# Gradient of the KV cache in a decode kernel: products over 64 rows and 512 columns per matmul instead of 32 rows and 256

One Trainium2 (trn2) chip, one core. The metric is the device time of one execution in microseconds (us), lower is better; a figure quoted for a kernel is the median of its runs.

## The reference

Two layers of grouped-query attention over a long cache alternate with two MLP layers, for two sequences of one token each, forward and backward. Ten outputs are asked: the result and the gradients of the input, the two caches and the weights.

```python
B, Sq, D = 2, 1, 1024
Hq, Hkv, Sk, Dh = 32, 4, 16384, 128          # 8 query heads per cache head

q = (x @ wq).reshape(B, Sq, Hq, Dh)...
scores = einsum("bhqd,bhkd->bhqk", q, k) * Dh ** -0.5
p = softmax(scores);  o = einsum("bhqk,bhkd->bhqd", p, v)
# ... wo, MLP; the same two layers twice with the same weights and caches
out, vjp = jax.vjp(f, x, k_cache, v_cache, wq, wo, w1, b1, w2, b2)
return (out, *vjp(grad_out))
```

What matters here: for each of the 8 pairs of sequence and cache head ("group", `g`), dV is P^T dO and dK is dS^T q, with 16 rows to sum over (2 layers x 8 heads) and 16384 tokens to produce. dK and dV together are 67 MB to write.

## The kernel before

Most loads of the caches and the weights, the forward pass and the first part of the backward pass come first, to about 733 us. The main loop after it loads another 50 of the 226 pieces of 1 MB of the caches, computes, for chunks of 32 tokens x 128 partitions, dS of the first layer and the gradients of K and V, and works off the weight gradients in the gaps.

The coefficients of dV and dK (`e_all` and `dX`) are transposed into `blk`: 128 rows are 4 pairs of tokens x (2 layers x 8 heads x 2 tokens). So 32 rows hold the coefficients of one pair of tokens. The moving operand `Qm` is block-diagonal: for each of two tokens 16 rows of q (or dO) in 128 columns, and zeros elsewhere. One matmul of 32 rows and 256 columns then gives two tokens of 128 numbers for 128 partitions. `Qm` is made at each new group: DVE spreads the columns of q into a scratch tile `spr`, two matmuls by the identity transpose it, and a copy takes it out of PSUM.

```python
    for w in "VK":
        spr[w] = wrk.tile([128, 258], BF16, name="spr" + w)
        nc.gpsimd.memset(spr[w][:], 0.0)

    def q_make(w, g, bank):
        Qm = wrk2.tile([128, 2, 128], BF16, name="Qm" + w)
        for t in range(2):
            PE.matmul(bank[:, t * 128:(t + 1) * 128], lhsT=spr[w][:, t * 128:(t + 1) * 128], rhs=ident[:],
                      start=True, stop=True)
        evac_cast(Qm[:].rearrange("p a b -> p (a b)"), bank[:, 0:256], 256)
        qms[w, g] = Qm
    # ... cut
    def make_qm(w, g):
        q_spread(w, cols[w][:, g].rearrange("p l r -> p (l r)"), 0, 16)    # DVE, at once
        return lambda: q_make(w, g, mx())                                  # PE and copy, later in the pass
    # ... cut
    def kv_pair(w, i, h):                    # half a chunk of dV or dK: 0.5 MB
        # ... cut
        pss = [mx() for _ in range(4)]       # the four PSUM banks that all such work shares
        for b in range(2):
            for r in range(4):
                PE.matmul(pss[r][:, b * 256:(b + 1) * 256], lhsT=blk[32 * r:32 * r + 32, o + 2 * h + b, :],
                          rhs=Qm[32 * r:32 * r + 32, :, :].rearrange("p a b -> p (a b)"), start=True, stop=True,
                          tile_position=(32 * r, 0))
        for r in range(4):
            evac_cast(sv_[:, 2 * h:2 * h + 2, r], pss[r][:].rearrange("p (b t d) -> p b t d", b=2, t=2), 512)
        # ... store
    # ... cut: the main loop, one pass
        for w, i in (("V", iv), ("K", ik)):
            if i is not None and chunks[i][1] == 0 and (w, chunks[i][0]) not in qms:
                qs.append(make_qm(w, chunks[i][0]))
        for k in range(2):
            ...                              # transpose, score block, one kv_pair
        for f in qs:
            f()
```

`evac_cast` gives a copy to ACT or DVE, whichever has less charged to it. In the orders of time shown below the copies and matmuls of an engine start in the order of the program (at the new group at 771.39 us, say, DVE's multiplication for dX starts at 772.05, the copy behind it at 772.64 and V's spreading at 773.24). A new group falls in every eighth pass, for V and K in the same pass, seven times in the loop.

Of the kernel before, what the change touches and what calls it, by code (L numbers as in the profile page):

```python
# [9 lines left out]
BF16 = mybir.dt.bfloat16  # L10
F32 = mybir.dt.float32
# [12 lines left out]
def kernel(  # L24
# [24 lines left out]
    nc = tc.nc  # L49
    V = nc.vector  # L50
    S = nc.scalar
    PE = nc.tensor
# [9 lines left out]
    FJ = F // 128  # L62
# [23 lines left out]
    wrk = ctx.enter_context(tc.tile_pool(name="wrk", bufs=1))  # L86
    wrk2 = ctx.enter_context(tc.tile_pool(name="wrk2", bufs=2))
# [20 lines left out]
    ident = const.tile([128, 128], BF16, name="ident")  # L108
# [25 lines left out]
    def charge(eng, us):  # L134
        load[eng] += us
# [7 lines left out]
    def pick():  # L143
        if only["e"]:
            return only["e"]
        m = min(load.values())
        for k in load:
            load[k] -= m
        return "A" if load["A"] <= load["D"] else "D"
# [9 lines left out]
    def evac_cast(dst, src, n):  # L159
        if pick() == "A":  # L160
            S.copy(out=dst, in_=src)  # L161
            charge("A", 0.17 + n / 1200.0)
        else:
            V.tensor_copy(out=dst, in_=src)  # L164
            charge("D", 0.15 + n / 960.0)
# [636 lines left out]
    def mlp_slope(l):  # L802
        sv = saved[f"m{l}"]
        hpre, th = sv["hpre"], sv["th"]
        t2 = wrk.tile([128, FJ, 2], F32, name="gb_t2")
        V.tensor_tensor(out=t2[:], in0=th[:], in1=th[:], op=ALU.mult)
        V.tensor_scalar(out=t2[:], in0=t2[:], scalar1=-1.0, scalar2=1.0, op0=ALU.mult, op1=ALU.add)
        x2 = wrk.tile([128, FJ, 2], F32, name="gb_x2")
        V.tensor_tensor(out=x2[:], in0=hpre[:], in1=hpre[:], op=ALU.mult)
        V.tensor_scalar(out=x2[:], in0=x2[:], scalar1=3.0 * GELU_A * GELU_C * 0.5, scalar2=GELU_C * 0.5,  # L810
                        op0=ALU.mult, op1=ALU.add)
        V.tensor_tensor(out=x2[:], in0=x2[:], in1=hpre[:], op=ALU.mult)
        V.tensor_tensor(out=x2[:], in0=x2[:], in1=t2[:], op=ALU.mult)
        d1 = sv["d1"] = vec.tile([128, FJ, 2], F32, name=f"gb_d1{l}")
        V.tensor_scalar(out=d1[:], in0=th[:], scalar1=1.0, scalar2=0.5, op0=ALU.add, op1=ALU.mult)
        V.tensor_tensor(out=d1[:], in0=d1[:], in1=x2[:], op=ALU.add)
# [105 lines left out]
    x3 = attn_layer_fwd(1, x2_)  # L922
    mlp_hidden(1, x3)
    mlp_slope(1)

    mlp_hidden_bwd(1, dh_up1)
# [16 lines left out]
    def some(q, n):  # L943
        for _ in range(n):
            if q:
                q.popleft()()

    mlp_slope(0)
    copies_on("A")
    g2 = attn_in_bwd(1, g3, dn1, lambda: some(rest, 2), lambda: some(rest, 3))  # L950
# [60 lines left out]
    cols = {}  # L1011
# [4 lines left out]
                V.tensor_copy(out=cols[w][:, :, k, :], in_=saved["a%d" % k]["qT_bf" if w == "K" else "doT_bf"][:])  # L1016
    g0_ = order[0]
    qms, spr, wide_do = {}, {}, {}
    for w in "VK":
        spr[w] = wrk.tile([128, 258], BF16, name="spr" + w)  # L1020
        nc.gpsimd.memset(spr[w][:], 0.0)

    def q_spread(w, gcols, k0, n):
        diag = spr[w][:].rearrange("p (t x) -> p t x", x=129)[:, :, 0:128].rearrange(
            "p t (r k z) -> p t r k z", r=4, k=16)[:, :, :, k0:k0 + n, 0]
        for t in range(2):
            V.tensor_copy(out=diag[:, t], in_=gcols.unsqueeze(1).to_broadcast([128, 4, n]))

    def q_make(w, g, bank):
        Qm = wrk2.tile([128, 2, 128], BF16, name="Qm" + w)  # L1030
        for t in range(2):
            PE.matmul(bank[:, t * 128:(t + 1) * 128], lhsT=spr[w][:, t * 128:(t + 1) * 128], rhs=ident[:],
                      start=True, stop=True)
        evac_cast(Qm[:].rearrange("p a b -> p (a b)"), bank[:, 0:256], 256)
        qms[w, g] = Qm

    def q_parts():
        q_spread("K", cols["K"][:, g0_].rearrange("p l r -> p (l r)"), 0, 16)
        q_make("K", g0_, px([128, 512], F32, "qk0"))
        q_spread("V", cols["V"][:, g0_, 1, :], 8, 8)  # L1040
        V.tensor_copy(out=wide_do[g0_][:, 8:16, 3], in_=cols["V"][:, g0_, 1, :])
# [77 lines left out]
    def nxt(what, lst):  # L1119
        rot[what] += 1  # L1120
        return lst[(rot[what] - 1) % len(lst)]

    def mx():
        return nxt("x", X)
# [4 lines left out]
    def new_home():  # L1129
        return (by_read or by_store).popleft()  # L1130
# [6 lines left out]
    def store(out_ap, view, tile_):  # L1137
        pace["queue"].dma_start(out_ap, view)
        if tile_ is not None:
            by_store.append(tile_)  # L1140
# [98 lines left out]
    late, late_pe = deque(), deque()  # L1239

    def make_qm(w, g):
        q_spread(w, cols[w][:, g].rearrange("p l r -> p (l r)"), 0, 16)
        return lambda: q_make(w, g, mx())

    stgs, split = {}, {}

    def kv_pair(w, i, h):

        g, c = chunks[i]
        if h == 0:  # L1250
            stgs[w, i] = new_home()
        sv_ = stgs[w, i][:].rearrange("p (b r t d) -> p b r t d", r=4, t=2, d=128)
        blk, Qm = blks[w, i], qms[w, g]
        o = 0 if w == "V" else NB
        pss = [mx() for _ in range(4)]
        for b in range(2):
            for r in range(4):
                PE.matmul(pss[r][:, b * 256:(b + 1) * 256], lhsT=blk[32 * r:32 * r + 32, o + 2 * h + b, :],  # L1258
                          rhs=Qm[32 * r:32 * r + 32, :, :].rearrange("p a b -> p (a b)"), start=True, stop=True,
                          tile_position=(32 * r, 0))  # L1260
        for r in range(4):
            evac_cast(sv_[:, 2 * h:2 * h + 2, r], pss[r][:].rearrange("p (b t d) -> p b t d", b=2, t=2), 512)
        if h == 0:
            split[w, i] = pace["short"] or i >= NC - 2
        if h == 1 or split[w, i]:
            lo = h if split[w, i] else 0
            dst = (dVv if w == "V" else dKv)[g, :, c * TC + lo * TC // 2:c * TC + (h + 1) * TC // 2, :]
            store(dst, stgs[w, i][:, lo * LDW // 2:(h + 1) * LDW // 2].rearrange("p (t d) -> p t d", d=128),
                  stgs[w, i] if h == 1 else None)
# [123 lines left out]
    dl_bank = delta_mm(0, dof, pt([128, 512], F32, "dl"), halves[1])  # L1393
    q_spread("V", dof[:, g0_], 0, 8)
    q_make("V", g0_, mx())
    V.tensor_copy(out=wide_do[g0_][:, 0:8, 3], in_=dof[:, g0_])
    odp = {1: kept_scores(1, sm_dp())}
    do_scaled(0, pairs(dops, HQ), dof, wob, (0,))
    delta(0, dl_bank, halves[1])
    charge("D", 1.0)  # L1400
    kv_pair("V", 0, 0)
    odp[0] = kept_scores(0, tp_dp())
    for c in (1, 0):
        ds0(c, odp[c])
    kv_pair("V", 0, 1)
    odp[2] = kept_scores(2, tp_dp())
    for q in range(4):
        dq_quad(1 - q // 2, q % 2)
    odp[3] = kept_scores(3, sm_dp())
    for c in (2, 3):  # L1410
        ds0(c, odp[c])
    kv_pair("V", 1, 0)
    for q in range(4):
        dq_quad(2 + q // 2, q % 2)
# [19 lines left out]
    while 2 * m < NS + 2:  # L1434
# [4 lines left out]
# [4 lines that stand above are left out]
            s = 2 * m + k  # L1443
            if s < NS:
                i, b = NCH + s // NB, s % NB
# [16 lines left out]
            at, w, m_ = ((k_at, "K", m - 1), (v_at, "V", m))[k]  # L1462
# [21 lines left out]
    i, g = NC - 1, order[-1]  # L1484
# [58 lines left out]
```

## Time and profile before

| | before |
|---|---|
| time, first three runs | 1142.25 us (1141.24 to 1142.84) |
| span of the profiled run | 1136.9 us |
| PE / DVE / ACT busy | 944.5 / 633.7 / 564.7 us |
| moved by DMA | 449.31 MB |
| calls of `kv_pair` | 128, from 733.5 to 1121.5 us |
| loop, passes 0 to 14 (14 passes; the engines set the pace) | 86.6 us |
| loop, passes 14 to 54 (40 passes; memory is full) | 256.4 us |
| from pass 54 to the end | 49.4 us |

The page of a profile describes one execution. The busy time of an engine says how long it had anything in hand, not that it was the limit: matmuls overlap in the trace (the eight of the call at 1018.53 us start within 130 ns and take 267 to 279 ns each). The row of GB/s against its own highest value, 425, is the better view of memory. A pass begins where the first transpose of its score block starts. Lines named L1258 and so on are lines of the kernel; the copies of all PSUM banks carry the lines of their helper, L161 on ACT and L164 on DVE.

One caution for all that follows: the profiled execution of the kernel before was a quick one. It took 1138.65 us, 3.6 less than the median and less than each of the runs in the table, so its stretches may be a few us short.

### The profile page before, as it was taken

Reading aid. Unit: us, or ns where it says so; the run is one execution under the profiler, and the core shown is the slowest. Engines: PE = TensorE matmul, PEld = TensorE weight load, DVE = VectorE, ACT = ScalarE, POOL = GpSimd, SP = SyncE. Lnnn points to the kernel's source line nnn. Section 1 sums busy time; section 2 is a strip of 40 time slices with the busy share of each in tenths; the row PEclk is TensorE's granted clock in tenths of the full one; section 3 lists DMA queues with packets and bytes.
Section 4 is the critical chain, followed back from the end, with each engine's and each line's share of the span. In section 5 each row is a group of like instructions: output and inputs, shape, how many; then the busy total and the mean of one; then the engine's idle time right before and its main releaser. Section 6 shows DMA issues by size and latency. Waiting matters only on the chain.

```text
span 1136.9 us, 40053 instructions
## 1 busy us (share of the span) xinstructions
PE 944.5 (83%) x17566; PEld 730.9 (64%) x17567; DVE 633.7 (56%) x1356; ACT 564.7 (50%) x1415; POOL 70.9 (6%) x126
## 2 busy tenths in 40 slices
PE   4989895487879885899988689989898989999884
PEld 3867674487767665888876578855555555555551
DVE  1545451133545432554846454678877868786784
ACT  0535351022535340343554344667777767786673
POOL 0000000000000000000000000022111112111210
PEclk9989796596999876899998799998987868896895
DMA  8999999998999989999999999998999999999996
GB/s 370 424 425 423 425 424 413 409 378 354 424 425 423 425 310 413 408 369 411 367 422 418 351 359 355 346 378 318 376 421 423 421 419 421 421 422 420 423 423 256
DMA packets 91983, 449.31 MB, mean 395 GB/s; under 512 B 7318, under 2 KB 7318, under 8 KB 54688
## 3 DMA queue, kind: packets, MB, share of 16 engines
q1 hardware_dynamic: 74448, 354.46, 77.4%
q0 software_dynamic: 17360, 92.29, 19.7%
q8 instruction: 137, 2.24, 0.7%
q14 instruction: 38, 0.31, 0.1%
HBM read 348.14 MB, written 98.58 MB: 393 GB/s over the span
## 4 chain that ended last, share of the span: by engine, by line
PE 55%; DMA 23%; DVE 11%; ACT 6%; issue 4%; POOL 0%; DVEq 0%; ACTq 0%; POOLq 0%
DMA kv_V<-in_A_v_cache_dram 13%; PE tp L420 10%; PE tpm L1450 5%; PE wtp L270 5%; PE acc_all L452 4%; PE xm L1258 4%; PE xm L1175 3%; DMA wt<-in_A_wo_dram 3%; PE sc L573 3%; DMA kv_K<-in_A_k_cache_dram 3%; PE dp L1312 3%; PE turn L322 3%; DMA keepK<-in_A_v_cache_dram 2%; PE dp L672 2%; DVE big L164 2%
## 5 line engine op out<-in xcount | busy, mean ns | idle before, releaser
L153 ACT COPY kT<-tp 128x512 int32<-128x512 int32 x209 | 122.6, 586 | 253.6 <-PE tp L420 242.5
L156 DVE COPY kT<-tp 128x1024 bf16<-128x1024 bf16 x159 | 108.6, 691 | 110.0 <-PE tp L420 97.8
L420 PE MATMUL tp<-ident,kv_K 128*128 128x128 bf16 x1728 | 145.5, 234 | 4.3 <-DMA kv_K<-in_A_k_cache_dram 4.2
L420 PEld LDWEIGHTS <-kv_K 128*128 128x128 bf16 x1728 | 110.2, 104 | 5.1 <-DMA kv_K<-in_A_k_cache_dram 4.8
L164 DVE CAST big<-xm 128x512 bf16<-128x512 f32 (+1 forms) x125 | 81.2, 686 | 24.6 <-PE xm L1258 16.8
L573 PEld LDWEIGHTS <-kT 128*128 128x128 bf16 x2048 | 76.6, 98 | 28.1 <-issue 21.9
L573 PE MATMUL sc<-qT_bf,kT 128*128 128x8 bf16 x2048 | 92.2, 172 | 0.9 <-issue 0.7
L161 ACT CAST big<-xm 128x512 bf16<-128x512 f32 (+1 forms) x139 | 75.6, 593 | 25.2 <-PE xm L1258 16.2
L420 PE MATMUL tp<-ident,kv_V 128*128 128x128 bf16 x864 | 70.8, 229 | 10.7 <-DMA kv_V<-in_A_v_cache_dram 9.0
L270 PE MATMUL wtp<-ident,wt 128*128 128x128 bf16 x928 | 74.8, 227 | 3.4 <-issue 2.2
L537 ACT ACTIVATE e_all<-sc,negm 128x64 bf16<-128x64 f32 x256 | 77.0, 344 | 1.3 <-DVE negm L532 1.2
L306 PEld LDWEIGHTS <-wt 128*128 128x128 bf16 x1696 | 48.9, 103 | 44.3 <-issue 14.9
L161 ACT CAST keepV<-xm 128x512 bf16<-128x512 f32 x116 | 63.5, 595 | 24.1 <-PE xm L1258 18.4
L452 PE MATMUL acc_all<-kv_V,e_all 128*16 128x256 bf16 x864 | 45.6, 291 | 25.5 <-DVE acc_all L435 12.3
L156 DVE COPY wT<-wtp 128x1024 bf16<-128x1024 bf16 (+1 forms) x64 | 40.7, 641 | 46.6 <-PE wtp L270 43.0
L153 ACT COPY wT<-wtp 128x512 int32<-128x512 int32 (+1 forms) x60 | 34.2, 571 | 62.5 <-PE wtp L270 48.2
L164 DVE CAST keepV<-xm 128x512 bf16<-128x512 f32 x88 | 56.9, 685 | 14.1 <-PE xm L1258 9.5
L164 DVE CAST keepK<-xm 128x512 bf16<-128x512 f32 (+1 forms) x86 | 55.8, 685 | 16.1 <-PE xm L1258 10.8
L420 PEld LDWEIGHTS <-kv_V 128*128 128x128 bf16 x864 | 55.8, 102 | 11.7 <-DMA kv_V<-in_A_v_cache_dram 9.7
L161 ACT CAST keepK<-xm 128x512 bf16<-128x512 f32 (+1 forms) x96 | 52.0, 592 | 16.7 <-PE xm L1258 15.2
L537 ACT ACTIVATION_READ_ACCUMULATOR e_all<-sc,negm 128x1 f32 x256 | 60.2, 236 | 0.0
L270 PEld LDWEIGHTS <-wt 128*128 128x128 bf16 x928 | 57.2, 101 | 4.1 <-issue 2.7
(366 smaller groups left out, 1785.0 us busy)
## 6 DMA issues: line engine op xcount, KB each, us to landing
kv_K<-in_A_k_cache_dram SPq DMA_DIRECT2D x81, 1024.0 KB, 11.8
kv_V<-in_A_v_cache_dram SPq DMA_DIRECT2D x81, 1024.0 KB, 12.2
wt<-in_A_wo_dram SPq DMA_DIRECT2D x32, 1024.0 KB, 10.3
wt<-in_B_w_dram SPq DMA_DIRECT2D x32, 896.0 KB, 14.1
out_dram<-big POOLq DMA_DIRECT2D x25, 1024.0 KB, 16.8
out_dram<-keepK POOLq DMA_DIRECT2D x18, 1024.0 KB, 19.8
wt<-in_A_wq_dram SPq DMA_DIRECT2D x16, 1024.0 KB, 9.0
wt<-in_B_w_dram SPq DMA_DIRECT2D x14, 1024.0 KB, 12.9
```

The costliest lines, as they stand in the source:

```text
L153: S.copy(out=dst.bitcast(I32), in_=src.bitcast(I32))
L156: V.tensor_copy(out=dst, in_=src)
L161: S.copy(out=dst, in_=src)
L164: V.tensor_copy(out=dst, in_=src)
L270: PE.transpose(tp[:, o, :], wv[:, j, (o0 + o) * 128:(o0 + o + 1) * 128], ident[:])
L306: PE.matmul(fps[:, jo, :].rearrange("p (a b) -> p a b", b=2), lhsT=wv[:, j, jo * 128:(jo + 1) * 128], rhs=xT_bf[:, j0 + j, :].unsqueeze(1) ...
L420: PE.transpose(tp[:, j, :], cv[:, b * 8 + j, :], ident[:])
L452: PE.matmul(self.acc[cg:cg + 16, :], lhsT=coef(u), rhs=self.cv[:, t:t + 2, :].rearrange("p t d -> p (t d)"), start=False, stop=True, tile_ ...
L537: S.activation(out=e_all[:, g, f * half:(f + 1) * half, l, h, :], in_=sc[g][f][:, h, :].rearrange("p (a b) -> p a b", b=2), func=ACT.Exp, ...
L573: PE.matmul(sc[g][f][:, :, t % TH], lhsT=kT[:, j, :], rhs=q_bf[:, g, :], start=True, stop=True)
L1258: PE.matmul(pss[r][:, b * 256:(b + 1) * 256], lhsT=blk[32 * r:32 * r + 32, o + 2 * h + b, :], rhs=Qm[32 * r:32 * r + 32, :, :].rearrange(" ...
L1450: PE.transpose(tp[:, j, :], cv[:, b * 8 + j, :], ident[:])
```

## The change

The intent: half as many matmuls and weight loads per call, and banks that are each filled by one matmul, so that its copy can start at once. The operand now holds four tokens: 64 rows (two pairs of tokens) and 512 columns. It is twice as large, so it needs space: V and K now share one scratch tile, spread only just before the matmuls that read it, and two scratch tiles of the MLP are shared.

```diff
-    for w in "VK":
-        spr[w] = wrk.tile([128, 258], BF16, name="spr" + w)
-        nc.gpsimd.memset(spr[w][:], 0.0)
+    spr["V"] = spr["K"] = wrk.tile([128, 512], BF16, name="spr")
+    nc.gpsimd.memset(spr["V"][:], 0.0)
 ... (q_spread: four copies instead of two)
     def q_make(w, g, bank):
-        Qm = wrk2.tile([128, 2, 128], BF16, name="Qm" + w)
-        for t in range(2):
+        Qm = wrk2.tile([128, 4, 128], BF16, name="Qm" + w)
+        for k in range(4):
 ...
     def make_qm(w, g):
-        q_spread(w, cols[w][:, g].rearrange("p l r -> p (l r)"), 0, 16)
-        return lambda: q_make(w, g, mx())
+        def f():
+            q_spread(w, cols[w][:, g].rearrange("p l r -> p (l r)"), 0, 16)
+            q_make(w, g, mx())
+
+        return f
 ...
-        for b in range(2):
-            for r in range(4):
-                PE.matmul(pss[r][:, b * 256:(b + 1) * 256], lhsT=blk[32 * r:32 * r + 32, o + 2 * h + b, :],
-                          rhs=Qm[32 * r:32 * r + 32, :, :].rearrange("p a b -> p (a b)"), start=True, stop=True,
-                          tile_position=(32 * r, 0))
-        for r in range(4):
-            evac_cast(sv_[:, 2 * h:2 * h + 2, r], pss[r][:].rearrange("p (b t d) -> p b t d", b=2, t=2), 512)
+        for k in range(4):
+            p = 64 * (k % 2)
+            PE.matmul(pss[k][:], lhsT=blk[p:p + 64, o + 2 * h + k // 2, :],
+                      rhs=Qm[p:p + 64, :, :].rearrange("p a b -> p (a b)"), start=True, stop=True, tile_position=(p, 0))
+        for k in range(4):
+            evac_cast(sv_[:, 4 * h + k, :], pss[k][:], 512)
```

More of the change, by code (lines that the diff above doesn't have):

```diff
@@ L804, in mlp_slope @@
         hpre, th = sv["hpre"], sv["th"]
-        t2 = wrk.tile([128, FJ, 2], F32, name="gb_t2")
+        t2 = wrk.tile([128, FJ, 2], F32, name="gb_t2", tag="g_z")
         V.tensor_tensor(out=t2[:], in0=th[:], in1=th[:], op=ALU.mult)
         V.tensor_scalar(out=t2[:], in0=t2[:], scalar1=-1.0, scalar2=1.0, op0=ALU.mult, op1=ALU.add)
-        x2 = wrk.tile([128, FJ, 2], F32, name="gb_x2")
+        x2 = wrk.tile([128, FJ, 2], F32, name="gb_x2", tag="g_rz")
         V.tensor_tensor(out=x2[:], in0=hpre[:], in1=hpre[:], op=ALU.mult)
@@ L1018 @@
     qms, spr, wide_do = {}, {}, {}
-    for w in "VK":
-        spr[w] = wrk.tile([128, 258], BF16, name="spr" + w)
-        nc.gpsimd.memset(spr[w][:], 0.0)
+    spr["V"] = spr["K"] = wrk.tile([128, 512], BF16, name="spr")
+    nc.gpsimd.memset(spr["V"][:], 0.0)
     def q_spread(w, gcols, k0, n):
-        diag = spr[w][:].rearrange("p (t x) -> p t x", x=129)[:, :, 0:128].rearrange(
-            "p t (r k z) -> p t r k z", r=4, k=16)[:, :, :, k0:k0 + n, 0]
-        for t in range(2):
-            V.tensor_copy(out=diag[:, t], in_=gcols.unsqueeze(1).to_broadcast([128, 4, n]))
+        diag = spr[w][:].rearrange("p (v t s y k z) -> p v t s y k z", v=2, t=2, s=2, y=2, k=16)
+        for v in range(2):
+            for t in range(2):
+                V.tensor_copy(out=diag[:, v, t, :, v, k0:k0 + n, t], in_=gcols.unsqueeze(1).to_broadcast([128, 2, n]))
     def q_make(w, g, bank):
-        Qm = wrk2.tile([128, 2, 128], BF16, name="Qm" + w)
-        for t in range(2):
-            PE.matmul(bank[:, t * 128:(t + 1) * 128], lhsT=spr[w][:, t * 128:(t + 1) * 128], rhs=ident[:],
+        Qm = wrk2.tile([128, 4, 128], BF16, name="Qm" + w)
+        for k in range(4):
+            PE.matmul(bank[:, k * 128:(k + 1) * 128], lhsT=spr[w][:, k * 128:(k + 1) * 128], rhs=ident[:],
                       start=True, stop=True)
-        evac_cast(Qm[:].rearrange("p a b -> p (a b)"), bank[:, 0:256], 256)
+        evac_cast(Qm[:].rearrange("p a b -> p (a b)"), bank[:, 0:512], 512)
         qms[w, g] = Qm
@@ L1251, in kv_pair @@
             stgs[w, i] = new_home()
-        sv_ = stgs[w, i][:].rearrange("p (b r t d) -> p b r t d", r=4, t=2, d=128)
+        sv_ = stgs[w, i][:].rearrange("p (k n) -> p k n", n=512)
         blk, Qm = blks[w, i], qms[w, g]
```

## The prediction

> **What bounds the kernel now.** I first asked where the changed code runs. The instructions of the dK and dV products (line L1258) start at 733.5 us and the last at 1121.5 us of a span of 1136.9 us; before that the change only adds a few small instructions. Then I read the page's slices, to see what runs full in that last third.
>
> ```profile
> PEclk9989796596999876899998799998987868896895
> GB/s 370 424 425 423 425 424 413 409 378 354 424 425 423 425 310 413 408 369 411 367 422 418 351 359 355 346 378 318 376 421 423 421 419 421 421 422 420 423 423 256
> ```
>
> No slice carries more than 425 GB/s, and ten of the last eleven stand at 419 to 423. So I cut the last 392 us by that row and asked for the engines' busy time in the three stretches (columns: stretch, length, PE, weight loads, DVE, ACT, POOL, granted clock, DMA share, GB/s).
>
> ```profile
> 745.00:836.00 91.00, 81.32 (x1208) 53.13 (x1208) 72.86 (x131) 67.50 (x131) 18.21 (x34) 0.91 0.96 366
> 836.00:1095.00 259.00, 232.15 (x3021) 142.61 (x3021) 201.64 (x352) 188.45 (x360) 42.70 (x69) 0.82 1.02 421
> 1095.00:1137.00 42.00, 24.36 (x255) 11.33 (x255) 23.07 (x47) 19.12 (x35) 1.07 (x2) 0.67 0.75 308
> ```
>
> I call them A, B and C. A moves 366 GB/s and its two copy engines are busy 80% and 74%: it is set by the engines. B moves 421 GB/s throughout: it is set by memory, or so nearly that a faster engine gains nothing. Its 259 us carry 109.1 MB, which at 423 GB/s is 258 us. C is the end, where DMA is not full and the chain runs through PE, copies and the last stores. The waits in B warn, though, that the balance is close: in all of B PE waits for a load only about 2 us, so engines that lose several per cent would become the bound.
>
> A pass of the main loop makes two half-megabyte pieces of dV or dK (one call each, 128 calls in all), two score blocks, and up to five matmuls of weight gradients. Each call has four PSUM banks, which DVE and ACT share two and two. How one call looks depends on whether its banks are free. Free, at full clock (start, length, engine):
>
> ```profile
> 1018.53 0.40 PE L1258 MATMUL xm<-QmK,blk 32*128 32x256 bf16 x8
> 1018.86 0.62 PE L1450 MATMUL tpm<-ident,keepV 128*128 128x128 bf16 x8
> 1018.95 1.07 ACT L161 CAST keepK<-xm 128x512 bf16<-128x512 f32 x2 [0.55 <-PE xm L1258]
> 1019.04 1.29 DVE L164 CAST keepK<-xm 128x512 bf16<-128x512 f32 x2
> ```
>
> PE gives it 0.33 us; the copies start 0.42 us after it, two per engine. And with banks still being emptied:
>
> ```profile
> 901.82 0.98 PE L1258 MATMUL xm<-QmV,blk 32*128 32x256 bf16 x8
> 902.78 1.07 ACT L161 CAST big<-xm 128x512 bf16<-128x512 f32 x2 [0.17 <-PE xm L1258]
> 902.80 1.29 DVE L164 CAST big<-xm 128x512 bf16<-128x512 f32 x2 [0.43 <-ACT kT L153]
> ```
>
> Each bank gets its second half only in the second round of four[...]. So no copy can start before the last of four banks is free: all four come at once, 0.96 us after the first matmul.
>
> [...] in one call at full clock four matmuls start at 900.621, .624, .627 and .697, the other four at .740 to .805. [...] The clock records of this trace have just the values 0.5 and 1.0, in steps of 3413 ns. [...]
>
> **The change part by part.**
>
> *PE time of a call.* Eight loads and eight matmuls of 32 rows and 256 columns, four at a time, become four and four of 64 rows and 512 columns, two at a time. An existing 512-column matmul shows the duration:
>
> ```profile
> L1258 PE MATMUL xm<-QmK,blk x512: 263/278/417, 745.0 to 1112.0; 32*128 32x256 bf16 x171
> L1175 PE MATMUL xm<-rowsB,rowsA x120: 371/372/605, 771.8 to 1066.1; 4*128 4x512 bf16 x120
> ```
>
> The 256 further columns take 372 - 263 = 109 ns, so 512 stream in about 215 ns. Columns in sequence per call go from 2 x 256 to 2 x 512: about +0.2 us at full clock, +0.4 us at half. That is 26 us of PE over 128 calls at full clock; in B it lies beside the transfers, unless PE becomes the bound.
>
> *Start of the copies.* With free banks the first two banks are full after one 512-column matmul, 0.37 us, against 0.385 us for the fifth of eight: no difference, and the other two (0.59 us) come before the copy engines, at 0.6 us a copy, want them. With busy banks each bank is finished by itself and its copy need not await the fourth. I sorted the 128 calls by the time between their first and last matmul start (over 0.42 us counts as waiting): 12 of 36 wait before 836 us, 15 of 82 in B, 7 of 10 in C. The idle time just before their copies, both engines together, is 0.87, 0.94 and 1.04 us a call. About 0.3 us of pass time may go in A and 0.5 in C: -3.6 us in A, -3.5 us in C.
>
> *Clock.* [...] half-clock windows fall from 5 of 26 to 2 in A, from 28 of 76 to 13 in B, 7 of 10 to 6 in C. A pass at half clock takes 7.2 us or so against 5.5, over two windows: 0.75 us a window, -2.3 us in A and -11 us of engine time in B.
>
> *The operand and its shared scratch.* At a new group, V and K used to be spread early in the pass into two scratch tiles. Now both use one, spread just before their matmuls, and K's spreading waits for V's matmuls. The order of the changed program shows on DVE four copies for V, then four for K, each with its waits. Before:
>
> ```profile
> 979.79 1.29 DVE L164 CAST keepxV<-xm 128x512 bf16<-128x512 f32 x2 [0.58 <-PE xm L1258]
> 980.50 0.27 PE L1032 MATMUL xm<-ident,sprV 128*128 128x128 bf16 x2 [0.77 <-ACT keepxV L161]
> 980.61 0.27 PE L1032 MATMUL xm<-ident,sprK 128*128 128x128 bf16 x2
> 980.72 0.39 PE L999 MATMUL tpm<-ident,e_all 128*128 128x128 bf16 x4
> ```
>
> After, V's copies can begin when DVE is free at 981.08, take about 4 x 0.17 us, then four matmuls (0.4), K's copies (0.7) and matmuls follow: PE reaches L999 at about 983.0, 2.3 us later. I take 2 us as lost for the pass, at seven switches, two of them in A: +4 us in A, +10 us of engine time in B. Twice the operand to copy and twice the spreading adds some 0.55 us per operand, some 1 us of pass time in A.
>
> **Sum.** A: +4 (switches) +1 (operand) +2.4 (PE: 24 calls with free banks x 0.2 us, half exposed) -3.6 (copies) -2.3 (clock) = +1.5 us. B: -11 (clock), +10 (switches), +8 or so of exposed PE, -5 (copies): about zero for the engines, while DMA cannot give over 1 us; I count 0. C: -3.5 us. Together -2 us: 1142.25 - 2 = 1140.
>
> **Rivals.** (1) *PE becomes the bound in B.* For it: PE is busy 90% there, and half-clock calls lengthen by 0.4 us. If the clock does not recover, 82 calls x 0.2 to 0.4 us give 16 to 33 us, a time of 1155 to 1170. Against: [...] transfers in flight long enough to bridge stalls of 2 us. (2) *The copies run free.* All waiting before copies and most half-clock windows vanish in A and C, and the switch costs little: A could fall to what its 33 MB need at 423 GB/s, 79 us, and C by 5: 1125. Against: two thirds of the calls gain nothing in their copies. (3) *Nothing moves*, because memory sets B and effects in A cancel: 1142.
>
> **Range and chances.** The terms of A and C are each uncertain by 2 to 4 us, B by -1 to +10. That gives 1128 to 1153. Faster by over 2% needs under 1119.4, more than A and C could give: 4%. Slower by over 2% needs 1165, rival 1 almost in full: 4%.
>
> **What would show it.** Calls with free banks should occupy PE for 0.5 to 0.6 us at full clock, with copies still starting some 0.4 us after. Calls with busy banks should show copies starting one by one. The granted clock in B should rise from 0.82 to about 0.9. At a switch PE should stand 2 us for DVE. B should remain at 421 GB/s; if it falls below 410, PE has become the bound and I am wrong upwards. If A shortens by over 5 us, the switch or the PE term was too large.

The sum came to +1.5 (A), 0 (B) and -3.5 (C), so -2 us and 1140. But two of its terms, -2.3 us in A and -11 us in B, stand as estimates only: they are (5 - 2) and (28 - 13) windows x 0.75 us. The counts before, 5 and 28, are read from the trace; the counts after, 2, 13 and 6, came from a rule that I had fitted to the trace of the kernel before. No run tests it; without these two terms A would come to +3.8 us and the engines in B to +13. A window is one step of the clock record of this trace, whose entries last 3.41 us or a multiple, but for the last. The times of a pass agree roughly with the trace: among the pairs of passes that start between 836 and 1080 us, the three at a mean clock of 0.55 to 0.57 took 13.1 to 15.0 us (6.6 to 7.5 a pass), the four at 0.98 to 1.0 10.4 to 10.7 us (5.2 to 5.4 a pass), though passes differ in what else they do. As to the transfers in flight: in the trace the loads of 1 MB of the caches into `keepV`, `keepK` and `big` take 9.3 to 15.0 us from issue to landing in the median, the stores of 1 MB from them 16.8 to 20.5 us.

## The result, and the profile after

The changed kernel is correct and takes 1142.3 us (1141.38 to 1145.03, four runs) against 1142.34 us of the kernel before (four runs): ratio 1.0005, 95% interval 0.9986 to 1.0024. Ratios are the mean time of one kernel's fast runs over that of the other's of the same rounds, so not quite the ratio of the medians quoted. A second set of rounds (after_again) gave 1141.11 us and 1.0007. So: the same.

Below that equality much has moved. First the same three stretches of the kernel after (columns as in the prediction; the first is the engines' stretch, the second the full one, the third the end; the last 2.8 us of this span, 1139.8 us, lie outside, and with them the third has a clock of 0.87 and 326 GB/s):

```profile
745.00:836.00 91.00, 78.03 (x1034) 48.13 (x1032) 69.89 (x138) 65.38 (x123) 17.34 (x31) 0.92 0.93 359
836.00:1095.00 259.00, 225.63 (x2654) 126.67 (x2651) 201.03 (x369) 188.16 (x358) 43.00 (x69) 0.90 1.02 420
1095.00:1137.00 42.00, 30.70 (x339) 14.72 (x336) 29.51 (x57) 25.74 (x49) 2.13 (x4) 0.90 0.85 347
```

In the middle the granted clock rose from 0.82 to 0.90 and weight loads fell from 143 to 127 us, yet the rate stands at 420 GB/s as before. In the first stretch less was moved, 359 GB/s against 366. By passes: 90.6 us (86.6 before) for the first fourteen, 258.6 (256.4) for the next forty, 44.2 (49.4) from there to the end; the first pair is to be read with the caution above.

Next the calls. All matmuls of the K calls (count: shortest/median/longest in ns):

```profile
L1260 PE MATMUL xm<-QmK,blk x256: 372/386/632, 747.3 to 1117.2; 64*128 64x512 bf16 x128
```

They last about as long as the 512-column matmul of the prediction (372 and 386 ns, shortest and median, against 371 and 372). Then the order of time of one call with free banks and, right after it, one whose banks are still being emptied:

```profile
1013.22 0.61 PE L1260 MATMUL xm<-QmK,blk 64*128 64x512 bf16 x4
1013.64 1.07 ACT L161 CAST keepxV<-xm 128x512 bf16<-128x512 f32 x2 [0.55 <-PE xm L1260]
1013.72 1.28 DVE L164 CAST keepxV<-xm 128x512 bf16<-128x512 f32 x2
1013.75 0.62 PE L1451 MATMUL tpm<-ident,keepK 128*128 128x128 bf16 x8
...
1014.57 0.86 PE L1260 MATMUL xm<-QmV,blk 64*128 64x512 bf16 x4
1014.60 0.60 ACT L153 COPY kT<-tpm 128x512 int32<-128x512 int32 x1
1015.02 1.29 DVE L164 CAST keepK<-xm 128x512 bf16<-128x512 f32 x2
1015.07 1.11 ACT L161 CAST keepK<-xm 128x512 bf16<-128x512 f32 x2
```

With free banks nothing is won: the copies start 0.42 us after the call, as before, and PE moves on after 0.53 us instead of 0.33. In the second call the matmuls wait for banks (0.86 us in all), but the copies of the banks that are done start after 0.45 us, not after 0.96 as in the call of the kernel before. For calls that waited for nothing (first and last matmul start at most 0.25 us apart) at full clock, the median time from a call's first matmul to the next work on PE is 538 ns after (85 calls) and 330 before (48 calls). Over all calls at full clock it is 538 and 517, because more of the calls waited before (40 of 88 against 27 of 112). At half clock it is 968 against 547 ns, but only 16 calls meet half clock, not 40.

Last, a new group (the order of time at the first of the seven):

```profile
771.39 0.61 PE L1260 MATMUL xm<-QmV,blk 64*128 64x512 bf16 x4
771.81 1.56 ACT L161 CAST big<-xm 128x512 bf16<-128x512 f32 x3 [0.46 <-PE xm L1260]
772.05 0.68 DVE L1321 TENSOR_TENSOR dX<-dp,e_all 128x512 bf16<-128x512 f32 x1
772.64 0.68 DVE L164 CAST big<-xm 128x512 bf16<-128x512 f32 x1
773.24 0.43 DVE L1026 COPY spr<-colsV 128x32 bf16<-128x32 bf16 x4
773.48 0.48 PE L1031 MATMUL xm<-ident,spr 128*128 128x128 bf16 x4 [1.48 <-DVE spr L1026]
774.07 0.69 DVE L164 CAST QmV<-xm 128x512 bf16<-128x512 f32 x1 [0.39 <-PE xm L1031]
774.67 0.43 DVE L1026 COPY spr<-colsK 128x32 bf16<-128x32 bf16 x4
774.91 0.49 PE L1031 MATMUL xm<-ident,spr 128*128 128x128 bf16 x4 [0.95 <-DVE spr L1026]
...
775.43 0.58 ACT L161 CAST QmK<-xm 128x512 bf16<-128x512 f32 x1 [2.06 <-PE xm L1031]
```

PE stands twice for DVE's spreading (1.48 and 0.95 us), because the spreading sits behind the multiplication that makes dX and a copy in DVE's order, and K's behind V's matmuls and copy. ACT then stands 2.06 us for want of a full bank. This first group is the worst of the seven: from the V call's first matmul to the transposes of L999 it is 2.73 to 3.85 us, 3.23 in the mean; in the kernel before the mean is 1.64.

In the middle stretch the waits for memory are now plain (waiting engine and line, what for, us in total, times, longest). After, then before:

```profile
PE acc_all L452 <- DMA keepV<-in_A_k_cache_dram: 8.0, 1, 8.0
DVE big L164 <- DMA out_dram<-big: 3.6, 1, 3.6
ACT big L161 <- DMA out_dram<-big: 3.1, 1, 3.1
```

```profile
PE tpm L1450 <- DMA keepK<-in_A_v_cache_dram: 2.1, 1, 2.1
ACT big L161 <- DMA out_dram<-big: 1.4, 1, 1.4
```

The engines after the change arrive ahead of memory and then stand for it: 8 us for one load, 3 to 4 us for stores that hold a buffer. Before, they hardly had to.

### The profile page after: what moved, and what is told of

Read it like the earlier page. It is cut to its first block, busy times and chain, and to the rows that moved or that the text cites. A ratio compares the mean times of both kernels' runs of the same rounds, so it can differ in the third digit from the quotient of the medians.

```text
span 1139.8 us, 38909 instructions
## 1 busy us (share of the span) xinstructions
PE 944.3 (83%) x17086; PEld 716.5 (63%) x17087; DVE 635.7 (56%) x1389; ACT 568.1 (50%) x1416; POOL 70.9 (6%) x125
## 4 chain that ended last, share of the span: by engine, by line
PE 54%; DMA 28%; DVE 10%; ACT 4%; issue 3%; POOL 0%; another core or an unknown queue 0%; ACTq 0%; DVEq 0%; POOLq 0%; SPq 0%
DMA kv_V<-in_A_v_cache_dram 10%; PE tp L420 10%; PE wtp L270 5%; PE tpm L1451 5%; PE xm L1260 4%; DMA kv_K<-in_A_k_cache_dram 4%; PE acc_all L452 4%; DMA wt<-in_A_wo_dram 3%; PE sc L573 3%; DMA wqt<-in_A_wq_dram 3%; PE turn L322 3%; PE dp L1313 3%; PE xm L1174 2%; DMA out_dram<-keepV 2%; DMA keepV<-in_A_k_cache_dram 2%
## 5 line engine op out<-in xcount | busy, mean ns | idle before, releaser
L161 ACT CAST big<-xm 128x512 bf16<-128x512 f32 x151 | 81.0, 593 | 21.0 <-PE xm L1260 11.4
L164 DVE CAST big<-xm 128x512 bf16<-128x512 f32 x113 | 73.3, 683 | 16.5 <-PE xm L1260 11.2
L270 PE MATMUL wtp<-ident,wt 128*128 128x128 bf16 x928 | 78.6, 234 | 3.7 <-issue 2.4
L306 PEld LDWEIGHTS <-wt 128*128 128x128 bf16 x1696 | 48.8, 103 | 44.5 <-issue 15.3
L420 PE MATMUL tp<-ident,kv_V 128*128 128x128 bf16 x864 | 68.4, 224 | 9.8 <-DMA kv_V<-in_A_v_cache_dram 8.7
L164 DVE CAST keepV<-xm 128x512 bf16<-128x512 f32 x88 | 56.9, 684 | 20.9 <-PE xm L1174 10.4
L270 PEld LDWEIGHTS <-wt 128*128 128x128 bf16 x928 | 60.2, 105 | 4.3 <-issue 2.9
## 6 DMA issues: line engine op xcount, KB each, us to landing
wt<-in_B_w_dram SPq DMA_DIRECT2D x14, 1024.0 KB, 13.4
```

Source lines behind the costliest of these rows:

```text
L161: S.copy(out=dst, in_=src)
L164: V.tensor_copy(out=dst, in_=src)
L270: PE.transpose(tp[:, o, :], wv[:, j, (o0 + o) * 128:(o0 + o + 1) * 128], ident[:])
L306: PE.matmul(fps[:, jo, :].rearrange("p (a b) -> p a b", b=2), lhsT=wv[:, j, jo * 128:(jo + 1) * 128], rhs=xT_bf[:, j0 + j, :].unsqueeze(1) ...
L420: PE.transpose(tp[:, j, :], cv[:, b * 8 + j, :], ident[:])
```

## The experiments

My theory (1): memory sets the middle stretch, so what the change gains there is hidden; the wait at a new group is paid in the first stretch, where the engines set the pace, and it eats what the early copies and the clock give there. The rivals: the engines set the middle stretch too and gains and losses happen to cancel there; or none of the parts is worth anything. Each run has, in the table, its median, its ratio to the kernel before in the same rounds, and of its profiled execution the granted clock and the three parts of the span. The rounds ran on several chips, so the ratios compare better than the medians. By the measure of 2% all of these are the same; the intervals show what smaller differences are clear of noise. The three parts come from one execution each, and like kernels differ in the first fourteen passes by 2 to 3 us (86.6 and 89.3 for the code of the kernel before).

| run | time us | ratio (95% interval) | clock | 14 passes | 40 passes | rest |
|---|---|---|---|---|---|---|
| before | 1142.25 | 1 | 0.857 | 86.6 | 256.4 | 49.4 |
| after | 1142.30 | 1.0005 (0.9986 to 1.0024) | 0.881 | 90.6 | 258.6 | 44.2 |
| own_scratch | 1137.36 | 0.9965 (0.9934 to 0.9996) | 0.884 | 85.8 | 257.7 | 47.9 |
| switch_alone | 1145.28 | 1.0028 (0.9995 to 1.006) | 0.847 | 92.9 | 261.5 | 45.2 |
| late_banks | 1150.31 | 1.0079 (1.0042 to 1.0115) | 0.871 | 94.8 | 263.3 | 43.0 |
| early_32 | 1137.59 | 0.9967 (0.9932 to 1.0001) | 0.853 | 82.9 | 257.6 | 49.1 |
| skew_32 | 1138.13 | 0.996 (0.994 to 0.9979) | 0.867 | 83.5 | 260.1 | 49.6 |
| after_again | 1141.11 | 1.0007 (0.9968 to 1.0045) | 0.880 | 90.7 | 262.0 | 42.3 |
| own_again | 1136.50 | 0.9966 (0.9932 to 1.0001) | 0.882 | 84.5 | 258.5 | 47.7 |

All of these give the right result. Five more have a table of their own below.

### own_scratch and own_again: the change without the shared scratch tile

```diff
-    spr["V"] = spr["K"] = wrk.tile([128, 512], BF16, name="spr")
-    nc.gpsimd.memset(spr["V"][:], 0.0)
+    for w in "VK":
+        spr[w] = wrk.tile([128, 512], BF16, name="spr" + w)
+        nc.gpsimd.memset(spr[w][:], 0.0)
...
-        def f():
-            q_spread(...)
-            q_make(w, g, mx())
-        return f
+        q_spread(...)
+        return lambda: q_make(w, g, mx())
```

The second tile needed space; six scratch tiles of the MLP's forward pass, each dead when the next but one is written, share two places for it.

> The changed kernel with a scratch tile of its own for V and for K again, spread early in the pass; the rest as changed. Theory 1 (memory sets the middle stretch; the wait at a new group costs the first stretch some 4 us and is absorbed later): 3 to 5 us under the changed kernel, ratio to the kernel before 0.996 to 0.998, PE no longer waits for the spreading copies, the middle stretch still at 420 GB/s. Rival (the engines set the middle stretch, all seven waits count): 10 to 14 us under, ratio 0.988 to 0.991. Rival (these waits lie beside other work): no difference, ratio 1.000.

1137.36 us, ratio 0.9965: 5 us under the changed kernel, as theory 1 has it. The first fourteen passes fall from 90.6 to 85.8 us, the middle still carries 421 GB/s, and ACT and DVE now stand 14.7 and 10.5 us for memory in the loop (3.1 and 3.6 in the changed kernel, 1.4 and 0.8 before). In the same place of the trace PE no longer waits for the spreading:

```profile
770.15 0.60 PE L1258 MATMUL xm<-QmV,blk 64*128 64x512 bf16 x4
771.21 0.38 PE L1032 MATMUL xm<-ident,sprV 128*128 128x128 bf16 x4 [0.46 <-ACT big L161]
771.70 0.38 PE L1032 MATMUL xm<-ident,sprK 128*128 128x128 bf16 x4
771.92 0.39 PE L999 MATMUL tpm<-ident,e_all 128*128 128x128 bf16 x4
```

From the V call to the transposes of L999 it is 1.77 us, against 775.23 - 771.39 = 3.84 us in the changed kernel: 2.07 us at this group, and some 1.5 us in the mean of all seven (1.77 against 3.23). The intervals of this run and of the changed kernel's, from different rounds, overlapped, so both went once more, side by side:

> The changed kernel once more, in the same rounds as own_again, because the intervals of its first runs (0.9986 to 1.0024) and of own_scratch (0.9934 to 0.9996), from different rounds, overlap. Theory 1: ratio to the kernel before 0.999 to 1.002, and 3 to 6 us over own_again. Rival (the wait at a new group costs nothing in the full kernel): equal to own_again.

> own_scratch once more, beside after_again: theory 1: ratio to the kernel before 0.995 to 0.998, 3 to 6 us under after_again, first 14 passes about 86 us against 90 to 91. Rival: equal to after_again.

1141.11 and 1136.5 us, ratios 1.0007 and 0.9966; first passes 90.7 and 84.5 us. The difference is 4.6 us again; side by side the six runs of own_again lie between 1134.2 and 1139.6 us and those of after_again between 1137.8 and 1143.7. That the medians and the first stretch repeat settles it for me, though the interval of own_again to the kernel before just touches 1.

### switch_alone: only the shared scratch tile, on the kernel before

```diff
-    for w in "VK":
-        spr[w] = wrk.tile([128, 258], BF16, name="spr" + w)
+    spr["V"] = spr["K"] = wrk.tile([128, 258], BF16, name="spr")
...  (make_qm as in the change: spread and matmuls together, late)
```

> The kernel before with one shared scratch tile spread late, as in the change, but 32 rows and 256 columns kept. Theory 1: 2 to 4 us over the kernel before, ratio 1.002 to 1.0035, from the two waits in the first stretch only. Rival (engines set the middle stretch): seven waits of 1.5 to 2 us, ratio 1.010 to 1.012. Rival (waits hidden): 1.000.

1145.28 us, 1.0028: the size that theory 1 gives, not the 1.010 of seven waits all paid; the interval (0.9995 to 1.006) alone would not exclude zero. The first fourteen passes took 6.3 us more than in the quick profile of the kernel before, above the 4 I had for it, but 3.6 more than in before_no_dk. The clock of its runs, 0.847 to 0.859, is that of the kernel before in these rounds (0.845 to 0.863), so a cost in clock is not shown. The middle is not free of the waits here: without any wait for memory of PE, DVE or ACT it carries 414 GB/s, and its 40 passes take 261.5 us against 256.4. A kernel whose engines are only just ahead of memory pays part of the wait there too.

### late_banks: the wide operand without the early banks

```diff
-        for k in range(4):
-            p = 64 * (k % 2)
-            PE.matmul(pss[k][:], ..., rhs=Qm[p:p + 64, :, :]...)
+        for v in range(2):
+            for k in range(4):
+                p = 64 * (k % 2)
+                PE.matmul(pss[k][:, v * 256:(v + 1) * 256], ..., rhs=Qm[p:p + 64, 2 * v:2 * v + 2, :]...)
```

> The changed kernel with each matmul of 512 columns cut in two of 256, all first halves before all second halves, so that no bank is full before the second round, as in the kernel before; array use per call stays doubled. If banks that fill one by one are worth something in the first and last stretch: 3 to 7 us over the changed kernel, ratio to before 1.003 to 1.006, the granted clock as in the changed kernel (0.88). If they are worth nothing: ratio 1.000 to 1.001, equal to the changed kernel.

1150.31 us, 1.0079, 8 us over the changed kernel, more than the upper end of what I expected. Fourteen passes 94.8 us, 4.2 more than the changed kernel. The middle takes 263.3 us (258.6 and 262.0 in the two profiles of the changed kernel) and carries 419 GB/s, without any wait for memory of PE, DVE or ACT in the loop: without early banks the engines no longer arrive ahead of memory. The granted clock of its six runs is 0.867 to 0.873, against 0.845 to 0.863 of the kernel before in the same rounds: raised by the wide operand, not by the order of the banks. This version also has eight matmuls and weight loads a call instead of four, but that costs PE little: 543 ns a call with free banks at full clock, against 538, and 968 at half clock in both.

### early_32 and skew_32: early banks without the wide operand

```diff
-        for b in range(2):
-            for r in range(4):
+        for r in range(4):
+            for b in range(2):
                 PE.matmul(pss[r][:, b * 256:(b + 1) * 256], ...)      # early_32
```

```diff
-        for b in range(2):
-            for r in range(4):
+        for r0 in range(0, 4, 2):
+            for b, r in ((0, r0), (0, r0 + 1), (1, r0), (1, r0 + 1)):
                 PE.matmul(pss[r][:, b * 256:(b + 1) * 256], ...)      # skew_32
```

> The kernel before with its eight matmuls in the order that fills one bank after the other (both halves of a bank before the next), still 32 rows and 256 columns. Granted clock as before, 0.86, if array use is what counts (it does not change). Banks one by one should give 3 to 6 us back in the first and last stretch[...]: ratio 0.997 to 1.002. If the rise of the clock in the changed kernel came from the order of the banks, the clock rises here too, to 0.87 or more.

> The kernel before (32 rows, 256 columns, two scratch tiles) with its eight matmuls two banks at a time: first halves of banks 0 and 1, their second halves, then banks 2 and 3. Banks fill early[...]. Theory 1 (copies that need not await the fourth bank are what helps in the first stretch, and memory sets the rest): as early_32 or 1 to 2 us better, ratio 0.993 to 0.997, first stretch of 14 passes 82 to 85 us against 86.6, clock as before (0.85 to 0.86). Rival (early_32's gain was luck of the runs, or came from its order on the rows): ratio 0.999 to 1.001.

Two lines exchanged in the kernel before give 1137.59 us (0.9967) and, with two banks at a time, 1138.13 us (0.996, interval 0.994 to 0.9979). The first fourteen passes fall to 82.9 and 83.5 us. The clock of early_32 is 0.849 to 0.854 in its six runs, as before, so the rise in the changed kernel does come from the wide operand. The clock of skew_32 is 0.867 in the profiled run, a little over what I expected, and 0.850 to 0.858 in the others. I had also counted some 0.2 us more of PE a call against early_32, and the time did not come: a call with free banks at full clock takes PE 340 ns in the median, against 330.

The middle stretch of skew_32 shows the limit once more (columns as above):

```profile
836.00:1095.00 259.00, 219.87 (x2961) 132.75 (x2958) 195.85 (x348) 183.55 (x354) 41.73 (x67) 0.86 1.01 420
```

PE is busy 12 us less there than before (232.15), and not one GB/s more comes of it.

### Five kernels with memory relieved

To see what the engines can do in the middle, five kernels leave out the stores of dK but for the last two chunks, some 31 MB. Their dK is wrong (output 2 is not written); all other outputs are right.

```diff
+            if w == "K" and i < NC - 2:
+                if h == 1:
+                    by_store.append(stgs[w, i])
+                return
             store(dst, stgs[w, i][...], stgs[w, i] if h == 1 else None)
```

> The kernel before without the stores of dK but for the last two chunks (wrong result on purpose, some 31 MB less to move), to see how fast its engines go in the middle stretch when memory is not full. Its engines waited for memory only about 4 us there, so they can gain little: theory 1: 5 to 15 us under the kernel before, ratio 0.987 to 0.996. If memory alone had held it: 50 us or more, ratio under 0.96.

> The changed kernel without the stores of dK but for the last two chunks (wrong on purpose). Theory 1 (the change does speed the engines up in the middle stretch, by the clock and the early copies, and memory hides it): 8 to 20 us under the same cut of the kernel before, ratio to the full kernel before 0.970 to 0.985, middle 40 passes well under 245 us. Rival (the longer matmuls and the waits for the spread operand eat what the clock gives): equal to the same cut of the kernel before, or slower.

> The changed kernel with own scratch tiles, without the stores of dK but for the last two chunks (wrong on purpose). All seven waits for the spread operand now lie where engines set the time: theory 1: 8 to 14 us under the same cut of the changed kernel, ratio to the full kernel before 0.960 to 0.977. Rival (the waits are absorbed by other work even there): under 3 us.

> early_32 without the stores of dK but for the last two chunks (wrong on purpose): banks that fill early, 32 rows, no change of the array's use. own_no_dk took 1098 us, before_no_dk 1129. If the early copies make the 31 us between them: about 1098 to 1105 here, clock as in before_no_dk (0.86). If the clock makes most of it: about 1120 here. I expect half: 1108 to 1118, ratio to the full kernel before 0.969 to 0.978.

> own_no_dk with its matmuls cut in two of 256 columns, second halves last, so that no bank fills early (wrong on purpose: no stores of dK): the doubled use of the array and its clock alone. If the early copies make the gain: about 1129, as before_no_dk, though its clock is 0.88 or more. If the clock makes most of it: about 1105. I expect 1115 to 1128, because the doubled columns cost 0.2 us a call here too: ratio 0.976 to 0.987.

| without most stores of dK | operand | banks | wait at a new group | time us | ratio to the full kernel before (95% interval) | 40 passes |
|---|---|---|---|---|---|---|
| before_no_dk | 32 rows | late | no | 1129.26 | 0.9894 (0.9869 to 0.9918) | 246.9 |
| early_32_no_dk | 32 rows | early | no | 1122.47 | 0.9776 (0.9702 to 0.985) | 250.0 |
| own_late_no_dk | 64 rows | late | no | 1126.50 | 0.9892 (0.9842 to 0.9943) | 244.3 |
| own_no_dk | 64 rows | early | no | 1098.28 | 0.9614 (0.9589 to 0.9639) | 230.7 |
| after_no_dk | 64 rows | early | yes | 1121.26 | 0.9806 (0.9774 to 0.9838) | 243.1 |

The middle stretch of before_no_dk, then of own_no_dk; neither reaches 420 GB/s any longer:

```profile
836.00:1095.00 259.00, 232.84 (x3153) 143.44 (x3152) 209.43 (x367) 196.63 (x375) 32.67 (x50) 0.87 0.92 351
```

```profile
836.00:1095.00 259.00, 239.43 (x2902) 133.11 (x2903) 221.56 (x414) 205.32 (x392) 31.84 (x49) 0.93 0.93 372
```

What follows. The kernel before gains only 13 us from 31 MB less, which memory alone at 423 GB/s would turn into 73: its engines were only just ahead of memory. The wide operand with early banks and without the wait is worth 31 us where memory does not hide it (1129.26 - 1098.28). The wait at a new group is worth 23 us there (1121.26 - 1098.28), more than 3 us a group and twice the 8 to 14 I expected: PE's stop of some 1.5 us is followed by copy engines that stand too (ACT for 2.06 us at the first new group of the changed kernel), and by windows at half clock (0.90 against 0.94 in a like stretch of 836 to 1050 us). The parts don't add up: early banks alone give 7 us by the medians and 13 by the ratios (the two came from different chips, so the ratios count), the wide operand alone 3 or nothing, both together 31. early_32_no_dk is the least certain of these: two of its runs took 1120.97 and 1123.97 us at a mean clock of 0.854, one 1108.4 us at 0.875, and one, 1125.24 us, counts as slow because of that fast one; in its profile (1123.97 us) the 40 passes were not faster than before_no_dk's. So where memory gives way, the clock of one and the same kernel may differ from run to run, and the time with it; which of the two follows the other is not shown. Of my expectations three missed in part: early_32_no_dk took longer than 1108 to 1118 us, though its ratio lies in the range; own_late_no_dk lies in its range of time, but its ratio of 0.9892 above 0.987; and the 40 passes of after_no_dk are not well under 245 us. The reading that fits is that the wide operand's longer matmuls cost PE what the clock gives unless the copies overlap them; that reading is argued, not shown.

## Why the prediction was right or wrong

The time was right (1140 predicted, 1142.3 measured, range 1128 to 1153), and so was the statement that memory hides the middle. Part of the closeness is luck: the end gains about what I credited to the early copies, but for another reason. The range, too, is not the sum of the uncertainties that stand beside it, which would be 1131 to 1158. Point by point:

- *PE time of a call: right, and in size.* Calls with free banks at full clock take 538 - 330 = 208 ns more; I took 0.2 us. At half clock +0.42 us, as predicted.
- *Start of the copies: right.* Free banks 0.42 us before and after; busy banks 0.45 instead of 0.96 us. The term of -3.6 us for the first stretch is what early_32 shows by itself, 86.6 - 82.9 = 3.7 us, and late_banks from the other side, 94.8 - 90.6 = 4.2; the like pairs without stores of dK show 89.3 - 85.0 = 4.3 and 89.9 - 84.8 = 5.1.
- *Clock: right in size; what in the new operand raises it is not shown.* 0.82 to 0.90 in the middle of the profiles, as announced, and over whole executions 0.842 to 0.863 in all runs of the kernel before and 0.871 to 0.881 in ten of the changed one; 15 of 76 windows at half clock there against 28 (13 predicted), 4 of 26 in the first stretch against 5 (2 predicted). All runs with operands of 64 rows lie at 0.867 to 0.904, those with 32 rows at 0.842 to 0.867, but for one at 0.875. PE's busy time does not go with it: 232 of 259 us in the middle before, at a clock of 0.82, and 226 after, at 0.90. The rule behind the predicted counts was my own estimate. The new operand fills twice the rows with each matmul, but it also streams longer, with two matmuls side by side instead of four (median starts in a call with free banks at full clock: 0, 3, 226 and 230 ns, against 0, 3, 7, 10 and 120 to 130 ns before), and no run separates the two.
- *The wait at a new group: right in kind, a little large for PE (2 us predicted, 1.5 measured in the mean of seven), too small in effect.* I counted +4 us in the first stretch; taking it away gave 4.8, 6.2 and, without stores of dK, 4.5 us (90.6 - 85.8, 90.7 - 84.5, 89.3 - 84.8). The spreading itself was cheaper than I wrote, 0.43 us for four copies and not 0.7, as they overlap (each takes some 0.18 us and they start about 0.085 us apart). What I left out is, I think, what follows when ACT and DVE run dry; that is argued.
- *The sum of the first stretch: right in sign, its size not settled.* +1.5 us was predicted. The profiles of the two kernels differ by 4.0, but that of the kernel before is the quick one, and before_no_dk and after_no_dk do not differ (both 89.3). The means of all profiles at hand, in none of which PE, DVE or ACT wait for memory in this stretch, are 88.0 (86.6, 89.3) before, 90.2 (90.6, 90.7, 89.3) with the change and 85.0 (85.8, 84.5, 84.8) with the change but without the wait: +2.2 us in all, of which the wait makes +5.2 (4 predicted) and the other terms -2.9 (4 - 1.5 = 2.5 predicted).
- *The engines in the middle: about right.* My terms sum to +2 us, not quite the zero I wrote, and the -5 for copies among them has no working. Where memory gives way the 40 passes are 3.8 us shorter with the change (246.9 to 243.1, one profile each).
- *The end: right in sign, wrong in reason.* I expected -3.5 us from early copies; the rest after pass 54 is 5.2 us shorter. But late_banks, without early copies, has the shortest rest of the full kernels but one (43.0), and early_32, with them, has 49.1, as before (49.4). What decides is what remains to be moved. Dividing the bytes left at 836 us by 423 GB/s gives 288.7 us before and 291.9 after, a difference of 3.2; the profiled spans differ by 2.9 (1139.8 - 1136.9). The remainder of the span is 12.2 and 11.9 us. For own_scratch, early_32, skew_32 and the two repeated runs it is 11.4 to 13.4; only switch_alone and late_banks, where PE, DVE and ACT never wait for memory in the loop, have more: 16.6 and 14.5. A kernel that comes late into the full stretch makes up for it at its end, and one that comes early waits there. So gains in parts of this loop don't add up to time.
- *Rival 1, PE as the bound in the middle: refuted.* The middle carries 420 GB/s, not under the 410 that I named as its sign, and after_no_dk is faster than before_no_dk by 8 us in spite of the waits, and own_no_dk by 31. *Rival 2, 1125 us: not reached*, by the wait and by memory; even without the wait it is 1137. *Rival 3* comes nearest to what happened, with the caution that what cancels is large: some 5 us for the wait against about as much for the rest.

Two versions beat the kernel before by more than the noise: own_scratch (the change with the wait removed), and skew_32, which is the kernel before with its eight matmuls in another order; early_32 gains as much, with an interval that touches 1. All gain about 4 to 5 us, so in the full kernel the wide operand adds nothing to early banks. Where memory gives way, own_no_dk is 24 us faster than early_32_no_dk by the medians and 18 by the ratios; skew_32 was not tried there. All of this rests on profiles of single executions for the split by passes; the start of the loop alone varies between 741.7 and 746.4 us among the full kernels, from the part before it that the change does not touch.

## What to carry to other kernels

When several matmuls fill several PSUM banks, order them so that each bank is finished as early as it can be: an order that finishes all banks in its last round makes the first copy wait for the last free bank (here 0.96 us after the call's first matmul, and 0.45 with the banks finished one by one), and here exchanging two loops was worth as much (some 5 us) as the whole redesign after its wait was removed; the redesign with the wait gained nothing. A larger operand that is paid for by sharing a scratch tile can lose on that tile what it gains: look where the shared tile's writer stands in its engine's order. And before crediting a faster engine, see whether memory is full in that stretch (here 420 GB/s, where no slice had more than 425), and test it by leaving out stores.
